# Loads held back until x is turned, and step 0's MLP continued by halves

## The chip, the cores and the metric

The kernel runs on one core of a Trainium2 chip. Its time is the device time of one execution in microseconds (us). Five engines run their own instruction queues in order: PE (matrix products), DVE and ACT (elementwise work), POOL (here small set-up work and the issue of software DMAs) and SP (the issue of hardware DMAs). They meet through semaphores. In the profile, "PEld" is PE's weight load, and "SPq" or "POOLq" is the issuing side of a queue.

## The reference

Windowed attention with sink tokens, and then an MLP with a rational activation, on the joined heads:

```python
batch, n_heads, seq, head_dim = (4, 8, 768, 64);  n_sink, window = (4, 128)
n_tokens, d_model, d_ff = (3072, 512, 2048)

scores = scale * np.matmul(q, k.transpose(0, 1, 3, 2))
keep = is_sink | ((rel >= 0) & (rel < window))     # rel = query position - key position
a = softmax(np.where(keep, scores, -1e9))
x = np.matmul(a, v)                                # as [B * S, H * D]

h = x @ w_in
P = a[0] + a[1] * h + a[2] * h**2 + a[3] * h**3
Q = 1.0 + np.abs(b[0]) * np.abs(h) + np.abs(b[1]) * h**2
out = (P / (Q + 1e-06)) @ w_out                    # float32, [3072, 512]
```

## The kernel before

The 3072 tokens are cut into 12 steps of 256 tokens (`TS`), three steps to a batch. A step s has an attention part and an MLP part, and the attention of later steps runs beside the MLP of earlier ones, about two steps ahead.

**Attention of a step.** POOL issues the loads, cast from float32 to bfloat16 on the way: two of k (`load_k`, L171, 128 KB each), two of q (`load_q`, L155), and eight of v, one a head (`load_v`, L179, 32 KB each). From step 3 on (from the seventh tile on for q) k and q are transposed by DMA, issued from SP: `turn_k_tile` (L335) into `kT_flat`, `turn_q` (L318) into `qT`; in the first steps PE does it. DVE spreads k into a block form (`spread_k`, L364). PE makes the scores of four head pairs (`scores`, L414) and of the sink tokens (`sink_scores`, L381), ACT takes the exponentials (`exps`, L432), DVE masks (`mask`, L439; in the first three steps PE adds the mask), PE multiplies with v in three units (`attend`, L468), and DVE divides (`normalize`, L481) into `x_n`. Then x is transposed into `xblk` in two halves: in steps 0 to 2 by PE (L492) and a copy on ACT (`place_x`, L501), from step 3 on by two DMA transposes from SP (`turn_x_half`, L504). A transposed k buffer has three copies, `v_bd` three, `k_bf` and `xblk` two each, `q_bf` four.

**MLP of a step.** `project_in` (L516) makes h in four quarters of 16 matmuls, copied out by ACT (`copy_in`, L523). Then, on 128 x 4096 elements: absolute values (`magnitude`, L546), squares (`square`, L540 on DVE, L538 on ACT), the denominator (`denominator`, L551), its reciprocal as exp(-ln) on ACT (`log_den`, L577; `recip_den`, L583), and on DVE `even` (L557), `odd` (L562), `odd_h` (L567), `numerator` (L571) and `gate` (L589), whose result g goes into `project_out` (L613): two tiles of tokens, each in two parts of 8 matmuls that need one half of g and one half of `w_out`. ACT copies out (`copy_out`, L618) and SP stores (`store`, L622). The denominator, the logarithm and the exponential go by halves of d_ff in each step; `even` to `gate` go over the whole width, except in the last step, which does them by halves too.

**The order.** The order of every engine's instructions is written by a planner in the kernel. Each operation is a `piece` with an engine, an estimated length, a rank, and a list of pieces that it follows. `run_list` (L900) plays a clock through: an engine that is free takes the able piece of the lowest rank. Where PE has nothing to do in that plan, it adds dummy matmuls (`spin`, L373), which multiply the identity into the bank of the scores. What comes out is a fixed order for each engine; on the chip each queue waits at its head for its own semaphores. The ranks of a step's loads are

```python
        r_ = 4 * s - 20
        ...
            piece(("load_v", s, h), "POOL", 0.62, r_ + 1.0, lambda s=s, h=h: load_v(s, h),
                  [("attend", s - 2, 2)] if s >= 3 else [("ones", s)], kind="sw", load=0.32)
```

and `w_out`'s 16 loads have the ranks -8.0 (the first eight) and -4.5. A load follows only what frees its buffer: k of a step follows the transposes of k two steps before, q those of q two steps before, v the attention two steps before.

Of the kernel before, what the change touches and what calls it, by code (L numbers as in the profile page):

```python
# [10 lines left out]
BF16 = mybir.dt.bfloat16  # L11
# [6 lines left out]
def kernel(  # L18
# [13 lines left out]
    nc = tc.nc  # L32
# [6 lines left out]
    P = 128  # L39
    DM = moe_w_in.shape[0]  # L40
    DF = moe_w_in.shape[1]
    NDMC = DM // P
    NFFC = DF // P
    NPB = H // 2
    TS = 256
    GPB = S // TS
    NSTEP = B * GPB
# [5 lines left out]
    MW = NFFC * TS  # L53
    HW = MW // 2
    NQ_HW = NTS + 1
# [119 lines left out]
    def load_v(s, h):  # L175
        b, g = divmod(s, GPB)
        v_bd[s] = v_fix[s % 3]
        i, e = divmod(h, 2)
        nc.gpsimd.dma_start(  # L179
            out=v_bd[s][e * 64:(e + 1) * 64, i, :, e, 0:D],  # L180
            in_=v[b, h, g * TS:(g + 1) * TS, :].rearrange("(j p) d -> p j d", p=64))
# [321 lines left out]
    def turn_x_half(s, grp):  # L503
        nc.sync.dma_start_transpose(  # L504
            out=x_half(s, grp).rearrange("p (u c) -> p u c", c=P),
            in_=x_n[s][:, 4 * grp * P:4 * (grp + 1) * P])


    hb, sq, den, num, g_of, lnq, ps_h, ps_out, o_t = {}, {}, {}, {}, {}, {}, {}, {}, {}

# [125 lines left out]
    def piece(name, eng, length, rank, run, after=(), takes=None, frees=None, lat=0.0, kind=None,  # L636
              load=0.0):
        w = Piece()
        w.name, w.eng, w.length, w.rank, w.run = name, eng, length, rank, run
        w.after = [a_ for a_ in after if a_ is not None]  # L640
        w.takes, w.frees, w.lat, w.kind, w.load = takes, frees, lat, kind, load
        w.order = len(work)
        assert name not in work
        work[name] = w
# [8 lines left out]
        return name + (s,) if 0 <= s < NSTEP else None  # L653


    piece(("load_k2",), "SP", 0.6, -22, load_k2, kind="hw", load=1.3)
    piece(("load_q3",), "SP", 0.6, -21, load_q3, kind="hw", load=2.8)
    for s in range(NSTEP):
        b, g = divmod(s, GPB)
        r_ = 4 * s - 20  # L660
        if s:
            for t in range(NTS):
                piece(("load_k", s, t), "POOL", 0.9, r_, lambda s=s, t=t: load_k(s, t),
                      [("turned_k", s - 2)] if s > 2 else [], kind="sw", load=0.88)
            for n in range(2 * s + 1, min(2 * s + 3, NQT)):
                piece(("load_q", n), "POOL", 0.9, r_ + 0.5, lambda n=n: load_q(n),
                      [("turn_q", n - 4) if n - 4 >= NQ_HW else None], kind="sw", load=0.88)
        for h in range(H):
            piece(("load_v", s, h), "POOL", 0.62, r_ + 1.0, lambda s=s, h=h: load_v(s, h),
                  [("attend", s - 2, 2)] if s >= 3 else [("ones", s)], kind="sw", load=0.32)  # L670
    for half in range(2):
        for c in range(NDMC):
            piece(("load_w_in", half, c), "POOL", 0.55, -18.9 + half * 3.6,
# [69 lines left out]
    for s in range(NSTEP):  # L743
# [19 lines left out]
        else:  # L763
# [5 lines left out]
        qts = [("place_q3", 1) if n < NQ_HW else ("place_q" if n < NQ_PE else "turn_q", n)  # L769
               for n in range(NTS * s, min(NTS * s + NTS + 1, NQT))]  # L770
        piece(("sink_scores", s), "PE", 0.45, 4 * s + 1 - 8 + 0.35, lambda s=s: sink_scores(s),
              [("spread_k", GPB * b)] + qts, takes="ps_m")
        piece(("sink_exps", s), "ACT", on_act(TS), 4 * s + 1 - 8 + 0.4, lambda s=s: sink_exps(s),
              [("sink_scores", s), ("attend", s - 2, 2) if s >= 2 else None], frees="ps_m")
        if g == 0:
# [44 lines left out]

    SQ_ACT = (4, 7, NSTEP - 1)
    RS = {0: 4.0, 1: 2.0}
    for m in range(NSTEP):
        r_ = 4 * m - RS.get(m, 0)
        old = m - 2
        for j in range(4):
            piece(("gemm1", m, j), "PE", 1.72, r_ + j, lambda m=m, j=j: project_in(m, j),
                  [("turned_x", m)] + [("load_w_in", j // 2, c) for c in range(NDMC)],
                  takes="ps_h")
            piece(("copy_in", m, j), "ACT", on_act(GW), r_ + j + 0.25,  # L830
                  lambda m=m, j=j: copy_in(m, j),
                  [("gemm1", m, j), ("odd_h", old) if old >= 0 and j == 0 else None], frees="ps_h")
        first, second = [("copy_in", m, 0), ("copy_in", m, 1)], [("copy_in", m, 2), ("copy_in", m, 3)]
        piece(("and", m, 0), "DVE", 0.6, r_ + 2.5, lambda m=m: magnitude(m, A_),
              first + ([("gate", old)] if old >= 0 else []))
        eng, how = ("ACT", "act") if m else ("DVE", "dve")
        piece(("sq", m, 0), eng, on_act(HW) if m else on_dve(HW, 2), r_ + 3.9,
              lambda m=m, how=how: square(m, A_, how), first + ([("num", old)] if old >= 0 else [("cast_k2",)]))
        piece(("and", m, 1), "DVE", 0.6, r_ + 4.2, lambda m=m: magnitude(m, B_),
              second + [("and", m, 0)])  # L840
        if m not in SQ_ACT:
            piece(("sq", m, 1), "DVE", on_dve(HW, 2), r_ + 4.25, lambda m=m: square(m, B_, "dve"),
                  second + [("sq", m, 0)])
        else:
            piece(("sq", m, 1), "ACT", on_act(HW), r_ + 4.25, lambda m=m: square(m, B_, "act"),
                  second + [("sq", m, 0)])
        for hf, part in ((0, A_), (1, B_)):
            piece(("den", m, hf), "DVE", on_dve(HW, 2), r_ + 4.35 + hf * 0.85,
                  lambda m=m, part=part: denominator(m, part), [("and", m, hf), ("sq", m, hf)])
            piece(("ln", m, hf), "ACT", on_act(HW, 0.2), r_ + 5.2 + hf,  # L850
                  lambda m=m, part=part: log_den(m, part),
                  [("more_scalars",), ("den", m, hf), ("exp", m - 1, hf) if m else None])
            piece(("exp", m, hf), "ACT", on_act(HW), r_ + 7.2 + hf,
                  lambda m=m, part=part: recip_den(m, part), [("ln", m, hf)])

        last = m == NSTEP - 1
        for hf, part in ((0, A_), (1, B_)) if last else ((None, None),):
            w_ = HW if last else MW
            x_ = 0.0 if hf is None else 1.5 * hf
            halves = (0, 1) if hf is None else (hf,)  # L860
            own = (m,) if hf is None else (m, hf)
            piece(("even",) + own, "DVE", on_dve(w_, 4, 0.12), r_ + 6.2 + x_,
                  lambda m=m, part=part: even(m, part),
                  [("sq", m, h_) for h_ in halves] + [("gate", m - 1) if m else ("cast_q3", 1)])
            piece(("odd",) + own, "DVE", on_dve(w_, 4, 0.12), r_ + 6.9 + x_,
                  lambda m=m, part=part: odd(m, part),
                  [("even",) + own] + [("den", m, h_) for h_ in halves])
            piece(("odd_h",) + own, "DVE", on_dve(w_, 2), r_ + 7.5 + x_,
                  lambda m=m, part=part: odd_h(m, part), [("odd",) + own])
            piece(("num",) + own, "DVE", on_dve(w_, 2), r_ + 7.6 + x_,  # L870
                  lambda m=m, part=part: numerator(m, part), [("odd_h",) + own])
            piece(("gate",) + own, "DVE", on_dve(w_, 2), r_ + 9.3 + x_,
                  lambda m=m, part=part: gate(m, part),
                  [("num",) + own] + [("exp", m, h_) for h_ in halves]
                  + ([("gemm2", m - 2, NTS - 1, 1)] if m >= 2 else
                     [("turned_k", 0), ("turn_q3", 1)]))
        for tt in range(NTS):
            bank = out_bank(m, tt)
            shared = bank == "ps_h"
            for part in range(2):  # L880
                f0, f1 = part * NFFC // 2, (part + 1) * NFFC // 2
                r2 = 0.5 * tt + 1.5 * part if last else 2 * tt + part
                piece(("gemm2", m, tt, part), "PE", 1.73, r_ + 10.6 + r2,
                      lambda m=m, tt=tt, f0=f0, f1=f1: project_out(m, tt, f0, f1),
                      [("gate", m, part) if last else ("gate", m)]
                      + [("load_w_out", c) for c in range(f0, f1)]
                      + ([("gemm2", m, tt, 0)] if part else [])
                      + ([("gemm2", m, 0, 0)] if shared and tt else []),
                      takes=None if part or shared and tt else bank)
            n = NTS * m + tt  # L890
            piece(("copy_out", m, tt), "ACT", on_act(DM), r_ + 12.8 + 2 * tt - 0.2,
                  lambda m=m, tt=tt: copy_out(m, tt),
                  [("gemm2", m, tt, 1), ("copy_out", m, 0) if shared and tt else None, ("store",) + divmod(n - 2, NTS) if n >= 2 else None],
                  frees=None if shared and not tt else bank)
            piece(("store", m, tt), "SP", 0.6, r_ + 12.8 + 2 * tt, lambda m=m, tt=tt: store(m, tt),
                  [("copy_out", m, tt)], kind="hw", load=0.7)
# [125 lines left out]
```

The softmax here doesn't subtract the row's maximum and nothing guards it: scores larger than these inputs give would overflow.

## Time and profile before

| | us |
|---|---|
| median of 5 runs | 272.29 |
| lowest and highest | 269.85, 273.75 |
| the profiled execution | 272.29 |
| its span | 270.6 |
| PE, DVE, ACT, POOL busy | 247.3, 230.4, 224.3, 121.6 |

The profile is of one execution. The span runs from the first to the last instruction; the rest of that execution's time, 1.7 us, lies around it. Busy times are sums over the span. A wait is listed with what ended it; the chain is followed back from the last instruction to what released it, step by step. PE's dummy matmuls count as busy: 395 of them are in the span, 30.1 us by their durations, which overlap.

### The profile page before, as it was taken

The numbers are of one execution on the slowest core, as the hardware profiler recorded it, in microseconds if no ns is written. First come the engines' busy times: TensorE is split into PE (matmuls) and PEld (weight loads), VectorE is DVE, ScalarE is ACT, GpSimd is POOL, SyncE is SP. The second block draws the span as 40 slices with busy tenths as digits, with TensorE's granted clock in tenths as the row PEclk, the third lists the DMA queues.
The fourth block names the chain that finished last, engine by engine and source line by source line (L and its number), as shares of the span: only waits on it lengthen the run. The fifth ranks groups of instructions, "written<-read, shape, count | busy, mean of one in ns | idle before, by whom it ended". The sixth has DMA issues, their size and how long they took to land.

```text
span 270.6 us, 5649 instructions
## 1 busy us (share of the span) xinstructions
PE 247.3 (91%) x2294; PEld 188.8 (70%) x2315; DVE 230.4 (85%) x293; ACT 224.3 (83%) x216; POOL 121.6 (45%) x178
## 2 busy tenths in 40 slices
PE   5899878998989759997989999999999999999994
PEld 5799777885776449877766777867858777675442
DVE  7975189869996298999998999999989999999950
ACT  8643858499979818799999999999999999899831
POOL 8945889799696496493924013290000000000000
PEclk9999999999999979999999999999999999999999
DMA  7999999999999999999995344491030211110222
GB/s 195 99 161 193 64 99 112 168 150 166 135 159 138 125 183 211 138 151 144 157 122 105 37 70 58 31 102 46 19 98 7 73 41 58 39 60 0 81 78 78
DMA packets 109674, 28.07 MB, mean 104 GB/s; under 512 B 101456, under 2 KB 105552, under 8 KB 109648
## 3 DMA queue, kind: packets, MB, share of 16 engines
q0 software_dynamic: 74288, 12.99, 73.7%
q1 hardware_dynamic: 35360, 14.72, 29.5%
q8 instruction: 18, 0.29, 0.5%
q14 instruction: 8, 0.07, 0.1%
HBM read 27.30 MB, written 6.29 MB: 124 GB/s over the span
## 4 chain that ended last, share of the span: by engine, by line
PE 54%; DMA 15%; ACT 9%; POOL 8%; DVE 6%; issue 4%; SPq 3%; ACTq 0%; POOLq 0%
PE ps_out L613 22%; PE ps_h L516 20%; DMA w_in_sb<-in_moe_w_in_dram 6%; PE ps_o L468 5%; DMA q_bf<-in_q_dram 4%; POOL v_bd L179 3%; PE ps_s L373 3%; PE ps_s L414 3%; DMA qT<-q_bf 3%; DMA xblk<-x_n 2%; ACT lnq L577 2%; ACT e L432 2%; SPq L318 2%; POOL w_out_sb L188 1%; ACT sq L538 1%
## 5 line engine op out<-in xcount | busy, mean ns | idle before, releaser
L516 PE MATMUL ps_h<-xblk,w_in_sb 128*128 128x256 bf16 x768 | 91.3, 275 | 4.8 <-DMA xblk<-x_n 4.6
L613 PE MATMUL ps_out<-w_out_sb,g 128*128 128x512 bf16 x363 | 86.8, 379 | 1.8 <-ACT o_t L618 0.6
L516 PEld LDWEIGHTS <-w_in_sb 128*128 128x128 bf16 x768 | 75.0, 99 | 17.8 <-issue 4.8
L179 POOL DMA_DIRECT2D v_bd<-in_v_dram x96 | 63.2, 681 | 45.0 <-PE ps_o L468 30.4
L613 PEld LDWEIGHTS <-g 128*128 128x128 bf16 x384 | 36.6, 98 | 37.0 <-issue 0.9
L523 ACT ACTIVATE hb<-ps_h 128x1024 bf16<-128x1024 f32 x48 | 49.7, 1042 | 12.9 <-PE ps_h L516 12.6
L577 ACT ACTIVATE lnq<-den,one_eps,qsc 128x2048 f32<-128x2048 bf16 x24 | 50.6, 2113 | 1.7 <-DVE den L551 1.6
L583 ACT ACTIVATE den<-lnq 128x2048 bf16<-128x2048 f32 x24 | 46.5, 1939 | 0.0
L432 ACT ACTIVATE e<-ps_s 128x768 bf16<-128x768 f32 x48 | 39.8, 834 | 7.0 <-PE ps_s L420 4.4
L373 PE MATMUL ps_s<-ident 128*128 128x128 bf16 x395 | 30.1, 226 | 6.8 <-ACT e L432 5.4
L551 DVE TENSOR_TENSOR den<-den,sq 128x2048 bf16<-128x2048 bf16 x24 | 29.1, 1220 | 3.1 <-ACT sq L538 2.8
L373 PEld LDWEIGHTS <-ident 128*128 128x128 bf16 x395 | 25.7, 102 | 8.3 <-issue 5.7
L468 PE MATMUL ps_o<-v_bd,e 128*128 128x130 bf16 x352 | 28.5, 219 | 0.1
L589 DVE TENSOR_TENSOR g<-num,den 128x4096 bf16<-128x4096 bf16 (+1 forms) x13 | 27.6, 2121 | 0.6 <-ACT den L583 0.5
L571 DVE TENSOR_TENSOR num<-num,sq 128x4096 bf16<-128x4096 bf16 (+1 forms) x13 | 27.6, 2122 | 0.1
L567 DVE TENSOR_TENSOR sq<-sq,hb 128x4096 bf16<-128x4096 bf16 (+1 forms) x13 | 27.6, 2120 | 0.1
L538 ACT ACTIVATE sq<-hb 128x2048 bf16<-128x2048 bf16 x14 | 27.1, 1938 | 0.1
L468 PEld LDWEIGHTS <-e 128*128 128x128 bf16 x352 | 24.5, 97 | 2.8 <-ACT e L432 0.2
L414 PE MATMUL ps_s<-qT,kT 128*128 128x192 bf16 x192 | 23.8, 246 | 1.8 <-DMA qT<-q_bf 1.2
L618 ACT ACTIVATE o_t<-ps_out 128x512 f32<-128x512 f32 x24 | 14.5, 614 | 12.3 <-PE ps_out L613 8.1
L171 POOL DMA_DIRECT2D k_bf<-in_k_dram x22 | 21.0, 967 | 5.9 <-DMA kT_flat<-k_bf 5.0
L155 POOL DMA_DIRECT2D q_bf<-in_q_dram x21 | 20.7, 996 | 5.1 <-DMA qT<-q_bf 4.6
(84 smaller groups left out, 239.0 us busy)
## 6 DMA issues: line engine op xcount, KB each, us to landing
out_dram<-o_t SPq DMA_DIRECT2D x24, 256.0 KB, 2.6
v_bd<-in_v_dram POOLq DMA_DIRECT2D x96, 32.0 KB, 4.6
k_bf<-in_k_dram POOLq DMA_DIRECT2D x22, 128.0 KB, 6.0
q_bf<-in_q_dram POOLq DMA_DIRECT2D x21, 128.0 KB, 6.3
w_in_sb<-in_moe_w_in_dram POOLq DMA_DIRECT2D x8, 256.0 KB, 8.5
w_out_sb<-in_moe_w_out_dram POOLq DMA_DIRECT2D x16, 128.0 KB, 5.1
stage_q<-in_q_dram SPq DMA_DIRECT2D x1, 768.0 KB, 6.3
stage_kv<-in_k_dram SPq DMA_DIRECT2D x1, 512.0 KB, 4.2
```

The source lines that it names most:

```text
L179: nc.gpsimd.dma_start(out=v_bd[s][e * 64:(e + 1) * 64, i, :, e, 0:D], in_=v[b, h, g * TS:(g + 1) * TS, :].rearrange("(j p) d -> p j d", p=64))
L373: nc.tensor.matmul(ps_scores[:, 0, 384:384 + P], lhsT=ident, rhs=ident, start=True, stop=True)
L414: nc.tensor.matmul(ps[:, n // 2, (n % 2) * 192:(n % 2) * 192 + 192], lhsT=kT_fix[s % 2][:, i * NHF + n, :], rhs=qT_fix[b % 2][:, i, c:c + ...
L432: nc.scalar.activation(out=data.rearrange("p (a n) c -> p a n c", a=2), in_=ps[:, :, 0:384].rearrange("p a (n c) -> p a n c", n=2), func=A ...
L468: nc.tensor.matmul(ps_o[:, u - u0, :], lhsT=l_, rhs=r_.rearrange("p e c -> p (e c)"), start=(m == 0), stop=(m == len(terms) - 1))
L516: nc.tensor.matmul(ps[:, n, :], lhsT=w_in_sb[c][:, fc * P:(fc + 1) * P], rhs=xblk[m][:, c, :], start=(c == 0), stop=(c == NDMC - 1))
L523: nc.scalar.activation(out=hb[m][:, j * GW:(j + 1) * GW], in_=ps_h.pop((m, j)).rearrange("p n c -> p (n c)"), func=AF.Copy)
L538: nc.scalar.activation(out=sq[m][:, c], in_=hb[m][:, c], func=AF.Square)
L551: nc.vector.tensor_tensor(out=den[m][:, c], in0=den[m][:, c], in1=sq[m][:, c], op=ALU.add)
L577: nc.scalar.activation(out=lnq[m, part], in_=den[m][:, c], func=AF.Ln, scale=qsc, bias=one_eps)
L583: nc.scalar.activation(out=den[m][:, c], in_=lnq[m, part], func=AF.Exp, scale=-1.0)
L613: nc.tensor.matmul(ps_out[m, tt], lhsT=g_of[m][:, co:co + P], rhs=w_out_sb[fc], start=(fc == 0), stop=(fc == NFFC - 1))
```

## The change

It has three parts.

1. A new piece, `touch`, for steps 0 to 8: a GpSimd copy of four elements (one partition) of `xblk` of that step into a scratch tile, which follows both transposes of x of that step. From step 4 on, the loads of k and q of step s follow the touch of step s - 4; from step 3 on, the loads of v follow the touch of step s - 3, and their rank is 2.6 higher than it was (`4 * s - 16.4` in place of `4 * s - 19`). POOL's queue is in order, so in the queue these loads stand behind the touch.
2. In step 0, too, `even` to `gate` are done by halves, and each part of the output product follows its half of g.
3. In the plan the sink scores of a step follow the last attention unit two steps before.

```diff
+    scratch = const_pool.tile([P, 4], BF16, name="scratch")
+
+    def touch_x(s):
+
+        nc.gpsimd.tensor_copy(out=scratch[0:1].rearrange("p (a b) -> p a b", a=2),
+                              in_=xblk[s][0:1, 0:NDMC:2, 0:TS:P])
...
+    LEAD = 4
+    for s in range(NSTEP - LEAD + 1):
+        piece(("touch", s), "POOL", 0.15, 4 * s - 9, lambda s=s: touch_x(s), [("turned_x", s)])
...
         r_ = 4 * s - 20
+        rv = r_ + 1.0 if s < LEAD - 1 else 4 * s - 16.4
         if s:
             for t in range(NTS):
                 piece(("load_k", s, t), "POOL", 0.9, r_, lambda s=s, t=t: load_k(s, t),
-                      [("turned_k", s - 2)] if s > 2 else [], kind="sw", load=0.88)
+                      [("turned_k", s - 2) if s > 2 else None,
+                       ("touch", s - LEAD) if s >= LEAD else None], kind="sw", load=0.88)
             for n in range(2 * s + 1, min(2 * s + 3, NQT)):
                 piece(("load_q", n), "POOL", 0.9, r_ + 0.5, lambda n=n: load_q(n),
-                      [("turn_q", n - 4) if n - 4 >= NQ_HW else None], kind="sw", load=0.88)
+                      [("turn_q", n - 4) if n - 4 >= NQ_HW else None,
+                       ("touch", s - LEAD) if s >= LEAD else None], kind="sw", load=0.88)
         for h in range(H):
-            piece(("load_v", s, h), "POOL", 0.62, r_ + 1.0, lambda s=s, h=h: load_v(s, h),
-                  [("attend", s - 2, 2)] if s >= 3 else [("ones", s)], kind="sw", load=0.32)
+            piece(("load_v", s, h), "POOL", 0.62, rv, lambda s=s, h=h: load_v(s, h),
+                  [("attend", s - 2, 2) if s >= 3 else ("ones", s),
+                   ("touch", s - LEAD + 1) if s >= LEAD - 1 else None], kind="sw", load=0.32)
...
         piece(("sink_scores", s), "PE", 0.45, 4 * s + 1 - 8 + 0.35, lambda s=s: sink_scores(s),
-              [("spread_k", GPB * b)] + qts, takes="ps_m")
+              [("spread_k", GPB * b), ("attend", s - 2, 2) if s >= 2 else None] + qts,
+              takes="ps_m")
...
+    BY_HALF = (0, NSTEP - 1)
...
         last = m == NSTEP - 1
-        for hf, part in ((0, A_), (1, B_)) if last else ((None, None),):
-            w_ = HW if last else MW
+        by_half = m in BY_HALF
+        for hf, part in ((0, A_), (1, B_)) if by_half else ((None, None),):
+            w_ = HW if by_half else MW
...
-                      [("gate", m, part) if last else ("gate", m)]
+                      [("gate", m, part) if by_half else ("gate", m)]
```

Since the planner plays its clock with the new pieces, the order changes in many places. On SP, the transposes around step 3's x stood in the order k(5), q(11), q(12), x(3, first half), k(6), q(13), q(14), x(3, second half). They now stand in the order k(5, first tile), x(3, first half), q(11), q(12), k(5, second tile), x(3, second half), q(13), q(14), k(6). On POOL, the last eight loads of `w_out` now stand ahead of the v loads of step 3, and the v loads of step 4 ahead of the k loads of step 5.

More of the change, by code (lines that the diff above doesn't have):

```diff
@@ L876 @@
                      [("turned_k", 0), ("turn_q3", 1)]))
+        if by_half:
+            for name in ("odd_h", "num", "gate"):
+                piece((name, m), "NONE", 0.0, 0, None, [(name, m, h_) for h_ in range(2)])
         for tt in range(NTS):
```

## The prediction

> **What bounds the kernel now.** Names: x(s,g) is the transpose of half g of the attention output of step s (L504), k(s,t) and q(n) are the transposes at L335 and L318, all three from SP. I read first the page's busy rows and slices, then the waits, the chain, the PE timeline at the largest wait, and the table by stage.
>
> ```profile
> span 270.6 us, 5649 instructions
> PE 247.3 (91%) x2294; PEld 188.8 (70%) x2315; DVE 230.4 (85%) x293; ACT 224.3 (83%) x216; POOL 121.6 (45%) x178
> PE   5899878998989759997989999999999999999994
> PEclk9999999999999979999999999999999999999999
> DMA  7999999999999999999995344491030211110222
> ```
>
> PE is the fullest engine. It has two soft places: the start, and slices 13 and 14 (88 to 101 us), where its clock drops too. The DMA engines are full until slice 20 (142 us) and light after.
>
> ```profile
> PE ps_h L516 <- DMA xblk<-x_n: 4.6, 1, 4.6
> DVE kT L364 <- DMA kT_flat<-k_bf: 4.9, 2, 4.7
> ACT o_t L618 <- DMA out_dram<-o_t: 4.2, 1, 4.2
> ```
>
> These waits (total, times, longest) fall together: three engines wait for DMAs at about 90 to 98 us. The chain and the PE timeline say what came last.
>
> ```profile
> 84.28 1.25 SPq L335
> 85.62 1.73 SPq L335
> 87.44 2.86 SPq L318
> 90.39 1.22 SPq L318
> 91.70 6.14 DMA xblk<-x_n
> 97.89 8.22 PE ps_h L516 x62
> ...
> 92.91 0.38 PE L516 MATMUL ps_h<-xblk,w_in_sb 128*128 128x256 bf16 x2
> 97.89 8.22 PE L516 MATMUL ps_h<-xblk,w_in_sb 128*128 128x256 bf16 x62 [4.60 <-DMA xblk<-x_n]
> ```
>
> x(3,1) was issued at 91.70, behind k(6,0), k(6,1), q(13), q(14), and took 6.14 us to land. Step 3's first product then ran 62 matmuls in 8.22 us; elsewhere 32 take 3.49 us on this chain (0.109 each), so 62 should take 6.76. The stall cost 4.60 + 1.46 us.
>
> ```profile
> core 0: us, PE busy (x) PEld busy (x) DVE busy (x) ACT busy (x) POOL busy (x), PEclk, DMA share, GB/s
> 110.00:130.00 20.00, 18.32 (x197) 15.30 (x196) 19.79 (x24) 18.67 (x18) 12.34 (x16) 1.00 1.95 144
> 150.00:170.00 20.00, 19.89 (x171) 15.19 (x171) 19.71 (x22) 19.70 (x19) 3.75 (x6) 1.00 0.35 51
> 210.00:230.00 20.00, 19.89 (x167) 14.50 (x167) 19.33 (x23) 19.98 (x18) 0.00 (x0) 1.00 0.19 55
> ```
>
> From 150 us on PE, DVE and ACT are all 97 to 100% busy. Nothing there can absorb a loss, and what all three gain before then should reach the end.
>
> **What the Trainium skill says.** "DMA: Bandwidth & Descriptors", section "Issuing engines are not separate DMA queues": DMAs from GpSimd and SP run on the same 16 engines and interleave. The trace agrees: transposes of turned x land in 3.4 us at the median, but the four issued between 82 and 99 us took 6.1 to 6.8 where landings are known, with POOL loads beside them. "Perfetto Trace Analysis", section on the HWDGE DMA instruction: the profiled interval of such a DMA ends with its issue, not with its data; 1.22 us of issue against 6.14 to landing above, so I count landings. "TensorE: Matmul & The Clock Gate", Part 1: an idle window of about 3.4 us halves the clock. The trace agrees: 4.60 idle, then the slow 62; waits of 1.4 us (at 36 us) left no such trace.
>
> **The change part by part.**
>
> *Step 0 by halves.* On DVE, five instructions become ten. Halves of the three products take 1217 to 1222 ns against 2284 for a whole (0.15 us more a pair), halves of the two scalings 0.81 against about 1.38 (0.24 more): 3 × 0.15 + 2 × 0.24 = 0.9 us. The first four halves (0.81 + 0.81 + 1.22 + 1.22 = 4.06 us) fit into a 5.48 us hole at 28.3 to 33.8, where DVE waits for step 1's attention, so they are free; were that hole gone they would cost their own 4 us. The second halves: from 41.3, with the two gates and a normalisation between them, g is whole at about 49.4 instead of 53.4. But the first output product of step 0 starts at 58.51 with PE busy before it, so g was not what it waited for. On PE itself, in the new order, the products of step 1 move ahead of one attention unit, and a turn of x moves ahead of ten or so dummy matmuls: I take 0.5 us (0 to 1).
>
> *The weights.* Loads of w_out 8 to 15 move ahead of step 3's eight v loads. Before, the last w_out landed at 64.1 and the second half of that output product began at 63.95; now about 59. The v loads are wanted at about 67 and issued by 60.8. Nothing is lost.
>
> *The touches.* Nine copies of four elements on one partition. No row shows one; nearest are memsets of 128x1 (0.10 us) and an affine select of 128x8 (0.20). I take 0.2 each (0.1 to 0.4), 1.8 us on a POOL that is 45% busy. They hold what stands behind them: k and q loads of step s+4, v loads of step s+3. Touches 0 to 2 find x turned or nearly so (the copy for step 2 ended at 66.96; POOL comes at about 67). Touch 3 waits for x(3,1), and then k(7), q(15), q(16), which POOL issued at 80.1 to 93.4, wait until then. That takes 4 loads of 128 KB out of the crowd around x(3,1), and as many per step later.
>
> *The queues.* POOL: all as before to q(10) (65.2 us); then eight v loads of step 4 stand ahead of k(5): 8 × 0.63 + a touch 0.2 + half of the 2.3 us of waits that they had = 6.3, so k(5) is issued at 71.5 to 73.2 (before: 65.1 to 67.6), q(11), q(12) by 75.0. Such loads landed in 4.2 to 7.2 us in this stretch; I take 5 to 5.5. SP: its new order is k(5,0), x(3,0), q(11), q(12), k(5,1), x(3,1), and only then q(13), q(14), k(6). k(5,0) can go at 76.5, and at 1.25 to 1.3 each x(3,1) is sixth: 76.5 + 5 × 1.25 = 82.8. Its source (third unit of step 3) is written by 82.2 or earlier. Landing 3.4 to 6.8 later; DMA work is still thick, so I take 5.9: 88.7.
>
> *PE there.* In the new order step 3's first product stands ahead of work that before was done by 92.9: two attention units of step 4 (0.85 + 0.57), an output half-tile of step 1 (2 × 1.73), three score products (3 × 0.33) = 5.87. So PE comes at 92.91 - 5.87 = 87.0 or a little less, with some 30 dummy matmuls in front, and waits under 2 us, too little to lose the clock. The sink scores of step 5, just ahead, need q(11) and q(12), which go by 81.5 and land by about 87 as well. To compare: before, with the slow clock added and that work and two early matmuls (0.22) taken out, 97.89 + 1.46 - 5.87 - 0.22 = 93.3; now 88.7. **Gain 4.6 us**; 6 if it lands at 87.3, 2.5 at 90.8. The 0.5 above is within this: the wait swallows it.
>
> *Afterwards.* Before, PE spends 85 dummy matmuls (4.8 us) and some 3 us of idle time between 120 and 147, behind a DVE that is 99% busy (110 to 130). DVE no longer loses 4.7 us to k(6), which now lands at about 93 when DVE comes at about 94. I take 1.2 us of those 7.8 (0 to 3.5). The added order of the sink scores behind an attention is the plan's own and costs nothing while PE has other work.
>
> Sum: 4.6 + 1.2 = 5.8. The profiled execution took 272.29 us, its span 270.6 and 1.7 around it; it is also the median of the five. 272.3 - 5.8 = **266.5 us** (span 264.8).
>
> **Rivals.** (1) *The stall only moves.* Up to q(14) POOL issues the same loads in both kernels, so the engines are as full when x(3,1) goes; if it lands at 93 or later PE waits 6 us again, with the slow clock. For it: share of DMA 2.44 in 76 to 92. Against: four fewer transposes and four fewer loads ahead of it. 93.3 - 93 = 0: 272. (2) *DVE or ACT keeps the time.* Both are full from 150 on; if the new order leaves them only half the gain, 272.3 - 2.9 = 269.4. For it: ACT 99.9% busy in 210 to 230. Against: ACT idles 4.2 + 1.8 us around 94 to 101 for the same cause. (3) *Slower: the loads come too late, in a ring.* Landing of x(s) releases four loads, whose q transposes stand ahead of x(s+1,1) on SP. Ring: touch 0.2 + loads 3.6 + landing 4.3 + two transposes 2.5 + own issue 1.2 + landing 3.4 = 15.2 us, against a step of 17.1 (the chain starts the products of steps 7 and 11 at 167.03 and 235.50). With landings as slow as at 81 us (9.8) and 99 us (6.8) it is 24.1, 7 over. It decides from 17.1 us on; at 18.9, five steps (4 to 8) lose 1.8 each: 272.3 - 5.8 + 9 = 275.5. Against: thinner traffic means landings as at 61 us (4.2).
>
> **How the numbers follow.** Forecast 0.60, (1) 0.12, (2) 0.16, (3) 0.12. The forecast's own range is 263 to 269. About 1% (2.7 us) is what a measurement of this kernel can tell from no change: faster is under 269.6. The forecast and two thirds of (2) are faster (0.70); the rest of (2) and (1) are within (0.17); (3) and an edge of (1) slower (0.13). The range reaches to (1): 263.0 to 272.8.
>
> **What would show it.** Right: x(3,1) issued near 83 and landed by 90; no PE wait over 3 us for turned x and no slow clock after 80; DVE's 4.7 us wait for k(6) gone; POOL idle before each touch from the fourth on. Wrong: waits of PE for turned x or q in steps 4 to 8 (rival 3), a DVE or ACT idle of the old size at another place (1), or a stall that is gone while PE idles more behind them (2).

## The result, and the profile after

The changed kernel takes 273.11 us (median of 43 runs, 269.8 to 276.5); the kernel before 272.14 (80 runs, 269.2 to 276.2). The ratio is 1.0024, 95% interval 1.0005 to 1.0042: no gain, where 266.5 us was forecast. Here and below a median is over all runs, while a ratio and its interval leave out the runs over 1.5% above the kernel's fastest, so the two can differ in the third digit. The profiled execution took 273.09 us, its span 271.4.

The page of the changed kernel:

```profile
span 271.4 us, 5660 instructions
PE 249.9 (92%) x2286; PEld 191.2 (70%) x2306; DVE 233.1 (86%) x298; ACT 224.6 (83%) x216; POOL 128.0 (47%) x187
PE   5999968894999899989998999999999999999994
PEclk9999979999799999999999999999999999999999
DMA  6999899999999999999899997975201211110222
```

The soft place at 88 to 101 us, with its slow clock, is gone. A new one stands in slice 9, counted from 0 (61 to 68 us), where PE is at 4 of 10, with the clock at 7 in the slice behind it. A smaller one, with the clock at 7 too, is in slice 5 (34 to 41 us): PE waits 2.16 us there for k(2). That one belongs to this execution; the kernels below with v first and with `w_out` cut, which are the same up to there, keep their clock. The waits (total, times, longest) name what is behind the one in slice 9:

```profile
PE ps_s L414 <- DMA qT<-q_bf: 3.4, 2, 2.3
DVE kT L364 <- DMA kT_flat<-k_bf: 3.7, 1, 3.7
POOL scratch L512 <- DMA xblk<-x_n: 24.9, 5, 5.7
POOL w_out_sb L188 <- DMA w_out_sb<-in_moe_w_out_dram: 3.7, 4, 1.4
POOL v_bd L179 <- DMA w_out_sb<-in_moe_w_out_dram: 3.1, 2, 1.6
```

PE waits for turned q, not for turned x. POOL, which issues the loads, now waits for `w_out` itself. The chain (start, length, what) and PE's timeline at that place:

```profile
47.48 8.97 DMA q_bf<-in_q_dram
...
56.46 1.19 SPq L318
...
57.74 9.05 DMA qT<-q_bf
...
66.83 0.33 PE ps_s L414 x2
67.15 2.92 PE ps_out L620 x8
```

```profile
65.34 0.34 PE L414 MATMUL ps_s<-qT,kT 128*128 128x192 bf16 x2 [2.25 <-DMA qT<-q_bf]
66.83 0.33 PE L414 MATMUL ps_s<-qT,kT 128*128 128x192 bf16 x2 [1.15 <-DMA qT<-q_bf]
```

The load of q(7) takes 8.97 us, the transpose of q(8) 9.05; the scores of step 3 wait 2.25 + 1.15 us, and the eight matmuls behind them take 2.92 instead of 1.73 (slow clock). That is 4.6 us; the stall that went cost 4.60 + 1.46 = 6.1, counted in the same way. Why q is late shows in the same stretch of POOL's queue, first in the kernel before, then in the changed one:

```profile
49.34 0.55 POOL L188 DMA_DIRECT2D w_out_sb<-in_moe_w_out_dram  x1 [0.33 <-DMA w_out_sb<-in_moe_w_out_dram]
50.48 1.26 POOL L179 DMA_DIRECT2D v_bd<-in_v_dram  x2 [0.59 <-PE ps_o L468]
52.46 3.97 POOL L179 DMA_DIRECT2D v_bd<-in_v_dram  x6 [0.71 <-PE ps_h L516]
56.40 1.12 POOL L188 DMA_DIRECT2D w_out_sb<-in_moe_w_out_dram  x2
57.78 3.04 POOL L188 DMA_DIRECT2D w_out_sb<-in_moe_w_out_dram  x5 [0.26 <-DMA v_bd<-in_v_dram]
60.79 1.80 POOL L171 DMA_DIRECT2D k_bf<-in_k_dram  x2
```

```profile
50.15 0.56 POOL L188 DMA_DIRECT2D w_out_sb<-in_moe_w_out_dram  x1 [0.89 <-DMA w_out_sb<-in_moe_w_out_dram]
51.85 1.07 POOL L188 DMA_DIRECT2D w_out_sb<-in_moe_w_out_dram  x2 [1.15 <-DMA w_out_sb<-in_moe_w_out_dram]
...
55.28 1.14 POOL L188 DMA_DIRECT2D w_out_sb<-in_moe_w_out_dram  x2 [1.40 <-DMA w_out_sb<-in_moe_w_out_dram]
...
58.16 2.47 POOL L179 DMA_DIRECT2D v_bd<-in_v_dram  x4 [0.29 <-PE ps_h L523]
62.13 1.42 POOL L179 DMA_DIRECT2D v_bd<-in_v_dram  x2 [1.50 <-DMA w_out_sb<-in_moe_w_out_dram]
65.15 1.22 POOL L179 DMA_DIRECT2D v_bd<-in_v_dram  x2 [1.60 <-DMA w_out_sb<-in_moe_w_out_dram]
67.30 1.77 POOL L171 DMA_DIRECT2D k_bf<-in_k_dram  x2 [0.94 <-DMA v_bd<-in_v_dram]
69.06 1.77 POOL L155 DMA_DIRECT2D q_bf<-in_q_dram  x2
```

Between the first of these `w_out` loads, which is w_out 8 in both kernels, and k(4) stand the same sixteen loads, and in the changed kernel one touch of 0.18 us. So seven loads of `w_out` moved, 9 to 15. Before, POOL gets through them in 60.79 - 49.34 = 11.45 us; now in 67.30 - 50.15 = 17.15. The loads themselves land later too: w_out 9 to 15 took 3.6 to 4.3 us from issue to landing before and 6.3 to 7.9 now, so that the last of them, issued 3 us earlier, lands at 65.2 instead of 64.1. k(4), q(9) and q(10), next on POOL, are 5.6 to 6.5 us later than before, and SP's queue for step 3 is late with them:

```profile
82.02 1.19 SPq L335 DMA_TRANSPOSE kT_flat<-k_bf  x1
83.39 1.19 SPq L504 DMA_TRANSPOSE xblk<-x_n  x1
84.67 2.62 SPq L318 DMA_TRANSPOSE qT<-q_bf  x2
87.38 1.22 SPq L335 DMA_TRANSPOSE kT_flat<-k_bf  x1
88.69 1.23 SPq L504 DMA_TRANSPOSE xblk<-x_n  x1
```

The order is the forecast one; each entry comes 5.5 to 6 us after its forecast time. PE at step 3's product:

```profile
94.23 1.39 PE L373 MATMUL ps_s<-ident 128*128 128x128 bf16 x22
95.46 1.98 PE L523 MATMUL ps_h<-xblk,w_in_sb 128*128 128x256 bf16 x16
```

x(3,1) took 6.7 us to land, until 95.4. PE comes out of its dummy matmuls at that moment: it doesn't wait because it is as late as x. By stage, first the line of the kernel before for 60 to 75 us, then the changed kernel:

```profile
core 0: us, PE busy (x) PEld busy (x) DVE busy (x) ACT busy (x) POOL busy (x), PEclk, DMA share, GB/s
60.00:75.00 15.00, 13.72 (x130) 10.24 (x131) 14.32 (x17) 14.38 (x15) 12.74 (x17) 1.00 1.84 152
60.00:75.00 15.00, 10.92 (x93) 7.49 (x91) 8.84 (x12) 9.95 (x10) 10.74 (x17) 0.89 1.50 106
150.00:170.00 20.00, 19.90 (x177) 15.26 (x178) 19.74 (x23) 19.38 (x19) 14.70 (x18) 1.00 1.49 121
210.00:230.00 20.00, 19.84 (x174) 14.88 (x176) 18.65 (x21) 19.35 (x19) 0.00 (x0) 1.00 0.18 51
```

From 150 us on it is nearly as full as before (93 to 100%). At 60 to 75 us all three engines lose: DVE is busy for 8.84 us instead of 14.32.

### The profile page after: what moved, and what is told of

Read it like the earlier page. It is cut to its first block, busy times and chain, and to the rows that moved or that the text cites. A ratio compares the mean times of both kernels' runs of the same rounds, so it can differ in the third digit from the quotient of the medians.

```text
span 271.4 us, 5660 instructions
## 1 busy us (share of the span) xinstructions
PE 249.9 (92%) x2286; PEld 191.2 (70%) x2306; DVE 233.1 (86%) x298; ACT 224.6 (83%) x216; POOL 128.0 (47%) x187
## 4 chain that ended last, share of the span: by engine, by line
PE 31%; DVE 19%; ACT 18%; DMA 17%; issue 7%; POOL 5%; another core or an unknown queue 1%; SPq 0%; ACTq 0%; POOLq 0%
PE ps_out L620 12%; PE ps_h L523 12%; DMA w_in_sb<-in_moe_w_in_dram 7%; ACT den L590 5%; ACT hb L530 4%; DMA qT<-q_bf 3%; DMA q_bf<-in_q_dram 3%; PE ps_o L468 3%; ACT lnq L584 3%; POOL v_bd L179 3%; DVE sq L574 3%; ACT e L432 2%; DMA k_bf<-in_k_dram 2%; DVE x_n L481 2%; ACT sq L545 2%
## 5 line engine op out<-in xcount | busy, mean ns | idle before, releaser
L620 PE MATMUL ps_out<-w_out_sb,g 128*128 128x512 bf16 x364 | 87.8, 383 | 1.6 <-ACT o_t L625 0.6
L432 ACT ACTIVATE e<-ps_s 128x768 bf16<-128x768 f32 x48 | 39.1, 819 | 10.1 <-PE ps_s L414 4.9
L373 PE MATMUL ps_s<-ident 128*128 128x128 bf16 x386 | 30.7, 233 | 6.6 <-ACT e L432 4.8
L373 PEld LDWEIGHTS <-ident 128*128 128x128 bf16 x386 | 26.9, 107 | 7.3 <-issue 4.5
L171 POOL DMA_DIRECT2D k_bf<-in_k_dram x22 | 21.6, 991 | 1.9 <-DMA v_bd<-in_v_dram 0.9
L414 PEld LDWEIGHTS <-kT 128*128 128x128 bf16 x192 | 16.9, 99 | 7.4 <-DMA qT<-q_bf 2.4
L481 DVE SCALAR_TENSOR_TENSOR x_n<-ps_o,csc,rec 128x384 bf16<-128x384 f32 (+1 forms) x36 | 20.6, 573 | 1.3
```

Of the source, the lines that this page charges most:

```text
L373: nc.tensor.matmul(ps_scores[:, 0, 384:384 + P], lhsT=ident, rhs=ident, start=True, stop=True)
L414: nc.tensor.matmul(ps[:, n // 2, (n % 2) * 192:(n % 2) * 192 + 192], lhsT=kT_fix[s % 2][:, i * NHF + n, :], rhs=qT_fix[b % 2][:, i, c:c + ...
L432: nc.scalar.activation(out=data.rearrange("p (a n) c -> p a n c", a=2), in_=ps[:, :, 0:384].rearrange("p a (n c) -> p a n c", n=2), func=A ...
L620: nc.tensor.matmul(ps_out[m, tt], lhsT=g_of[m][:, co:co + P], rhs=w_out_sb[fc], start=(fc == 0), stop=(fc == NFFC - 1))
```

## Experiments

Theory: the changed load order (`w_out` 9 to 15 ahead of step 3's v) makes q(7), q(8) and POOL's queue late, and this takes the gain. Rivals: DVE and ACT keep the time whatever PE does ("bound"); the halves or the touches cost it; the early waits do. The third part of the change, the sink scores behind an attention unit, stays in every kernel made from the changed one and isn't priced by itself. "Exchange" below means this edit, which leaves every engine's order as planned and swaps places on POOL alone (here v first; the other way round in the second kernel):

```diff
+    order = run_list()
+    moved = [("load_v", 3, h) for h in range(H)] + [("load_w_out", c) for c in range(9, NFFC)]
+    slots = [i_ for i_, w in enumerate(order) if w.name in moved]
+    for i_, name in zip(slots, moved):
+        order[i_] = work[name]
-    for w in run_list():
+    for w in order:
```

| kernel | median us | ratio to before | 95% interval |
|---|---|---|---|
| changed | 273.11 | 1.0024 | 1.0005, 1.0042 |
| changed, v first | 271.22 | 0.9964 | 0.9932, 0.9995 |
| before, w_out first | 274.55 | 1.0109 | 1.0049, 1.0169 |
| changed, q first | 275.25 | 1.0136 | 1.0063, 1.0208 |
| changed, no halves | 273.35 | 1.0031 | 0.9996, 1.0065 |
| changed, w_out cut | 269.46 | 0.9890 | 0.9860, 0.9919 |
| before, w_out cut | 271.28 | 1.0009 | 0.9983, 1.0035 |
| touches and halves | 269.53 | 0.9908 | 0.9879, 0.9937 |
| touch-only | 267.03 | 0.9824 | 0.9774, 0.9875 |
| touch-only, second set | 266.94 | 0.9814 | 0.9753, 0.9875 |
| touch-only, w_out first | 268.99 | 0.9927 | 0.9900, 0.9954 |
| before and halves | 270.06 | 0.9938 | 0.9909, 0.9967 |
| no halves, v first | 270.24 | 0.9950 | 0.9924, 0.9976 |

**The exchange in both kernels.**

> The changed kernel, every engine's order kept, but on POOL the eight v loads of step 3 exchange places with the loads of w_out 9 to 15, so that they stand ahead again as in the kernel before. Crowding (my theory: the weights beside them make q(7) and q(8) late): latencies of q(7), q(8) loads fall from 8.7-9.0 to 6.5-7.1 us and of their transposes from 8.8-9.1 to 5-6; PE's 3.4 us wait for q goes, with the slow clock after it; 267.5 to 269.5 us. Bound (rival: DVE and ACT keep the time whatever PE does): the wait goes and the time stays at 272 to 274. Early loss (rival: the 2.2 us wait for k(2) and the touch ahead of the last w_in load made PE late already): q no longer late but the time falls by no more than 1 us.

> The kernel before, every engine's order kept, but w_out 9 to 15 exchange places with the v loads of step 3 and stand ahead, as in the changed kernel. Crowding: q(7), q(8) loads and transposes take 8 to 9 us each instead of 5 to 7, PE waits 2 to 4 us for q at about 65 us, and the stall of step 3's product shrinks by what PE comes later, so the time grows by 0 to 4 us (272 to 276). If the weights don't crowd q: no wait for q over 1 us, latencies as before, 271.5 to 272.8 us.

With `w_out` first, the kernel before gets the changed kernel's stall at the changed kernel's place, and 1.1% (3.0 us):

```profile
64.06 0.34 PE L414 MATMUL ps_s<-qT,kT 128*128 128x192 bf16 x2 [2.68 <-DMA qT<-q_bf]
65.49 0.48 PE L414 MATMUL ps_s<-qT,kT 128*128 128x192 bf16 x2 [1.09 <-DMA qT<-q_bf]
```

The transpose of q(7) took 8.6 us there; in the kernel before 5.1, in the changed one 8.8. The stall at step 3's product stays beside it, smaller (2.69 us, at 101.34). With v first the changed kernel has q in time (5.0 us) and gains 0.6%, less than I expected, because PE's planned order now uses `w_out` 9 to 15 before they land:

```profile
63.10 0.38 PE L620 MATMUL ps_out<-w_out_sb,g 128*128 128x512 bf16 x1 [0.48 <-DMA w_out_sb<-in_moe_w_out_dram]
63.81 0.38 PE L620 MATMUL ps_out<-w_out_sb,g 128*128 128x512 bf16 x1 [0.34 <-DMA w_out_sb<-in_moe_w_out_dram]
64.53 0.38 PE L620 MATMUL ps_out<-w_out_sb,g 128*128 128x512 bf16 x1 [0.34 <-DMA w_out_sb<-in_moe_w_out_dram]
65.28 0.38 PE L620 MATMUL ps_out<-w_out_sb,g 128*128 128x512 bf16 x1 [0.38 <-DMA w_out_sb<-in_moe_w_out_dram]
66.07 0.58 PE L620 MATMUL ps_out<-w_out_sb,g 128*128 128x512 bf16 x1 [0.41 <-DMA w_out_sb<-in_moe_w_out_dram]
...
66.88 0.84 PE L414 MATMUL ps_s<-qT,kT 128*128 128x192 bf16 x4
```

Five matmuls wait for one load each, and the slow clock follows (four score matmuls in 0.84 us; 0.49 at full clock). In the changed plan PE comes to the second half of step 0's output product at 61.5 us, soon after the first; in the plan before it came at 63.95, and `w_out` at 64.1. So the change asked the DMA engines for q and for `w_out` at about 62 us; either order makes one of them late.

**q first.**

```diff
+    moved = [("load_q", 7), ("load_q", 8)] + [("load_w_out", c) for c in range(8)]
```

> The changed kernel, every engine's order kept, but on POOL the loads of q(7) and q(8) exchange places with w_out 0 to 7 and stand ahead of them, 4 to 5 us earlier. Crowding: the transposes of q(7), q(8) are issued about 4 us earlier, q is there when PE comes, the wait of 3.4 us goes; w_out 0 to 7 come 1.5 us later, still before 58 us; 267.5 to 270 us. Bound: 272 to 274 with the wait gone. Early loss: less than 1 us faster.

Slower still, 275.25 us: a miss. q is there, and from 60 to 75 us PE, DVE and ACT are busy again (13.7, 13.3 and 14.5 of 15). The loss comes behind: at 78.83 the scores of step 4 wait 1.97 us for DVE's spread of k, and at 95.59 step 3's product 2.10 us for x, with a slow clock in between. POOL came to k(4) at 64.37, after 60.79 in the kernel before, but ahead of the changed kernel's 67.30. Why this ends slower than the changed kernel stays open; that q in time isn't enough, it shows.

**Fewer bytes in the same places.**

```diff
-        nc.gpsimd.dma_start(out=w_out_sb[c], in_=moe_w_out[c * P:(c + 1) * P, :])
+        rows = P if c < 8 else 8
+        nc.gpsimd.dma_start(out=w_out_sb[c][0:rows], in_=moe_w_out[c * P:c * P + rows, :])
...
-rhs=w_out_sb[fc],
+rhs=w_out_sb[fc % 8],
```

> The changed kernel, every order kept; the loads of w_out 8 to 15 fetch 8 of their 128 rows, and the output products read w_out 0 to 7 in their place. This takes 8 loads of 128 KB out of the DMA engines at 50 to 60 us and leaves the order and the number of issues alone. Supply: q(7), q(8) loads land in 6.5 to 7.5 us, their transposes in 5 to 6, PE's wait of 3.4 us and the slow clock behind it go, and no other wait replaces them: 266 to 268.5 us, the time that I had forecast. Bound: 271 to 273 with the waits gone.

> The same cut of w_out 8 to 15 in the kernel before. Supply: nothing waits for these loads there, and the stall at 98 us comes from SP's queue and from loads issued after 70 us, so it stays at 3 to 5 us: 270.5 to 272.5 us, so that the changed kernel with the same cut is 3 to 5 us faster than this one. If loads issued at 50 to 60 us push everything later, so that the whole queue comes forward: 268 to 270 and the stall is smaller.

This kernel leaves out 120 of 128 rows of these loads and multiplies with other rows in their place. The changed kernel gains 1.3 points of ratio and has no wait for q left, and POOL comes to k(4) at 61.55 instead of 67.30; the kernel before gains nothing and keeps its stall (3.34 us at 97.69). With this cut, the change is worth (1.0009 - 0.9890) × 272 = 3.2 us. That speaks against "bound": a supply cut of loads at 50 to 60 us reaches the end. It is a little short of the 266 to 268.5 expected; PE still waits 1.92 us for x at 91.48.

**The halves.**

```diff
-    BY_HALF = (0, NSTEP - 1)
+    BY_HALF = (NSTEP - 1,)
```

> The changed kernel without step 0 by halves (the planner orders the rest anew, touches and places of v as changed). My prediction priced the halves at a gain of 0.5 us (0 to 1), so 273 to 274 here. If the halves are what costs (ten DVE instructions for five, attention units shifted on PE): 270 to 271. If the crowding is all, w_out still stands ahead and the wait for q stays at 2 to 4 us.

No difference from the changed kernel (1.0031 to 1.0024). The halves are not what took the gain. But PE's wait for q is only 1.64 us here, less than expected and with the clock full, and the kernel is no faster for it. Nor is the wait always 3.4 us with the halves: two runs below that leave out touches and keep this load order show 1.82 and 1.97 us. So the 4.6 us above are one execution's, and the late q isn't the whole loss.

**Step 3's loads at their old rank, planned anew.**

```diff
-        rv = r_ + 1.0 if s < LEAD - 1 else 4 * s - 16.4
+        rv = r_ + 1.0 if s < LEAD else 4 * s - 16.4
...
-                   ("touch", s - LEAD + 1) if s >= LEAD - 1 else None], kind="sw", load=0.32)
+                   ("touch", s - LEAD + 1) if s >= LEAD else None], kind="sw", load=0.32)
```

> The changed kernel with step 3's v loads at their old rank and without their touch (the other touches, the halves and the sink scores stay), and the planner orders all anew: the v loads stand ahead of w_out 9 to 15, and on PE the second half of step 0's output product comes later again, behind three score products, an attention unit and two pieces of step 2's product. Unlike the run with the places exchanged on POOL alone, PE then meets neither a late q nor a late w_out. Supply (my theory now: at 45 to 70 us the DMA engines cannot deliver both q(7), q(8) and w_out 8 to 15 by the time at which the changed order uses them): no DMA wait of PE over 1.2 us between 55 and 80 us, clock full there, 267 to 269 us. Bound (rival: DVE and ACT keep the time): 271 to 273 with PE's waits gone.

> As the run before it, and without step 0 by halves: what is left of the change is the touches from step 4's k and q loads and step 4's v loads on. PE's order to 90 us is then that of the kernel before. Supply: the stall of 4.6 us and its slow clock at 98 us shrinks to under 2 us and nothing is lost ahead of it: 267 to 269 us. Halves count: if the halves are worth what I predicted (0.5 us), 0 to 1 us slower than the run before it. Bound: 271 to 273.

> Once more the kernel with the touches and the halves and step 3's v loads at their old place, whose six runs lay between 264.8 and 273.6 us, beside kernels of the same set. If the halves cost nothing: 266 to 268, as without them. If they cost what the medians so far say: 269 to 271.

The first of the three was too scattered to read: 264.8 to 273.6 in six runs, median 270.1, and a ratio of 0.9798 (0.9708 to 0.9889) that rests on two of them. Its repetition gives 269.5, slower than the 267 to 269 expected. Without the halves ("touch-only") it is 267.0 us, 1.8% faster than before and the best version found. (It also keeps the later rank of v from step 4 on and the order of the sink scores.) It differs from the kernel without halves (273.35 us) in these two lines alone: (1.0031 - 0.9824) × 272 = 5.6 us. Its step 3:

```profile
90.66 1.22 SPq L504 DMA_TRANSPOSE xblk<-x_n  x1
...
92.67 5.27 SPq L504 DMA_TRANSPOSE xblk<-x_n  x2
```

```profile
93.80 0.38 PE L523 MATMUL ps_h<-xblk,w_in_sb 128*128 128x256 bf16 x2
94.76 6.93 PE L523 MATMUL ps_h<-xblk,w_in_sb 128*128 128x256 bf16 x62 [0.58 <-DMA xblk<-x_n]
```

The 62 matmuls end at 101.69; before, they ended at 106.11, on the same PE order. x(3,1) is issued only a microsecond earlier than before (90.66; it was 91.70) and still behind k(6), q(13), q(14), but lands by 94.76, in 4.1 us instead of 6.14. Two things differ beside it: the transposes of k(7), which stood right behind it, now come behind x(4), and the loads of k(7), q(15), q(16) and, through the touch, of the next v come later. Without the touches, in the same order, x(3,1) takes 6.5 us (90.19 to 96.69), with v loads beside it; so in these traces the order alone doesn't make it land faster.

**The price of the exchange there, and of the plan.**

> The 267.0 us kernel (touches without the halves, step 3's v loads at their old place), every order kept, but w_out 9 to 15 exchange places with step 3's v loads on POOL, as in the changed kernel. This prices the load order alone in a kernel that has no other loss there. Supply: q(7), q(8) late, PE waits 1.5 to 4 us at 62 to 66, and with the slow clock the time grows by 2.5 to 5 us, 269.5 to 272. Planner (rival: the order that the planner makes after 80 us from the moved ranks costs the rest of the 6 us between this kernel and the one with the moved v loads): only 0 to 2 us slower.

> The changed kernel without the halves (273.4 us), every order kept, but step 3's v loads exchange places with w_out 9 to 15 on POOL and stand ahead. It differs from the 267.0 us kernel only in the order that the planner made of the moved ranks on the other engines (70 lines of PE's order differ). Loads alone: if the exchange is worth what it was in the other pairs (2.8 us) and the plan costs the rest: 270 to 271. Tied together (PE's order assumes the early w_out, so that PE then waits for w_out 9 to 15 instead, as in the same exchange in the changed kernel): 271.5 to 273. If the plan costs nothing: 267 to 268.

With `w_out` first, the touch-only kernel loses 1.0% (2.8 us) by waits of 1.45 and 1.56 us for q at 62.75 and 64.65. With v first, the kernel without halves gains 0.8% (2.2 us). That is the 270 to 271 of "loads alone". Between the latter and touch-only, which have these loads in the same order, 1.3% (3.4 us) remain, and the orders of the other engines are what differs. Which part of these orders costs it isn't shown. One part is seen: PE meets the late `w_out` again (five waits, 1.6 us, and the slow clock after).

**The halves alone.**

```diff
+    BY_HALF = (0, NSTEP - 1)
```

> The kernel before with step 0's products by halves and nothing else of the change. My prediction: a gain of 0.5 us (0 to 1), 271.5 to 272.3 us here. If the order that the planner makes of it costs time (second attention unit of step 1 and the dummy matmuls moved, x turned later): 273 to 276.

A gain of 1.7 us, more than forecast: in that plan PE has attention and output work left in front of step 3's product, which starts at 97.89 without a wait, x(3,1) having landed at 97.5. A smaller stall stays ahead of it (2.71 us at 90.68, for DVE's normalisation, with the slow clock behind it). Halves and touches work on the same stall, and their gains don't add: with the halves, by the repetition above, the touch-only kernel is 0.8 to 0.9% slower (by its ratio, the scattered first set shows no difference). PE there waits 2.14 us at 108.78 for x of step 4.

**The touches themselves.**

```diff
-        if w.run:
+        if w.run and w.name[0] != "touch":
```

> The changed kernel, every order kept, the nine touches left out. If their waits hold back loads that PE then lacks (my rival of the ring, or a cost of the touches themselves): 1 us or more faster, 271 to 272. If their waits protect the transposes of x: 1 to 3 us slower, 274 to 276. If only the order counts: 272.5 to 273.7.

> The same 267.0 us kernel, every order kept, but the nine touches are not issued, so that POOL goes on to the loads behind them as soon as their buffers are free. If it is the order of the queues that brings the gain (x(3,1) ahead of q(13), q(14) and k(6) on SP) and not the waits of the touches: 266 to 268 us, x(3,1) still issued by 84 us. If the waits bring it (loads of step 7 and later held back from the transposes): x lands 2 us or more later in steps 4 to 8 and the time is 269 to 272.

> The touch-only kernel, every order kept, the touches left out, once more, beside the kernel with them on the same chip. Order alone: within 0.7 us of it. Waits count: 1 to 2.5 us slower than it.

> The touch-only kernel again, as the base of this set: 266.5 to 268 us, ratio to the kernel before 0.979 to 0.986.

> The changed kernel, every order kept, without touches 0 and 1. If the cost lies with these two, among the weights' loads: 270 to 271 us, as without all nine. If it lies with the later ones: 272.5 to 273.7. If both early cost and late gain count: under 270.

> The touch-only kernel, every order kept, without touches 0 and 1. The late touches bring the gain: 265.5 to 267.2 us, no slower than with all nine. The early ones do: 268 to 269, as without all.

Touch-only without its touches takes 267.78 us (0.9894) and 268.59 us (0.9893, beside 266.94 with them): some 1.1% comes from the order alone. Another 0.7% may come from the waits, but the intervals overlap. x(3,1) isn't issued by 84 us, as the second text expected, but at 90.19, behind q(13), q(14) and k(6). Without touches 0 and 1 it is 267.84 (0.9837, 0.9803 to 0.9871), between the two forecasts: which touches help isn't told apart. In the changed kernel the sign turns: without any touch 270.44 us (0.9948, 0.9920 to 0.9976), 2 us faster; without the first two 272.78 (1.0062, 1.0020 to 1.0104), no faster. So touches 2 to 8 cost about 2 us there. Through which wait isn't settled: the profiles with and without them differ in several small places. In both of these runs PE comes earlier to step 3's product and waits for x, 1.87 and 1.80 us at 93.8 and 94.0, with the clock full.

## Why the prediction was wrong, step by step

- *The stall at step 3's product*: right in the mechanism, in part by luck in the trace. There is no wait for x, no slow clock after 80 us, and DVE's wait for k(6) is gone. But x(3,1) landed at 95.4, not 88.7, and PE happened to be as late. Where PE is in time, it waits 1.8 to 1.9 us (`w_out` cut, touches left out), within the "under 2 us" forecast. The 3.7 us that DVE still waits are for k(3), until 55.4 us; it waits as long with v first (3.76) and with `w_out` cut (4.33), so that isn't the load order's. That the stall is worth 4 to 5 us the touch-only kernel shows (4.4 at the end of that product, 4.8 to 5.1 in the time).
- *"The weights ... Nothing is lost"*: the step that failed. I asked only whether `w_out` and v come by when they are used, and took it that loads issued earlier land earlier: the last `w_out` at about 59 (it was 65.2, after 64.1 before), v issued by 60.8 (it was 66.4). Seven loads moved, not eight; w_out 8 stood ahead of v already. I didn't ask what runs beside these loads (the transpose of q(7): 5.1 us became 8.8) nor what stands behind them on POOL. Measured: 1.6 to 3.0 us by the exchange in four pairs, and 5.6 with the plan that follows from the moved rank, against nothing in my sum.
- *"POOL: all as before to q(10) (65.2 us)"*: failed by the same cause. The issue of q(10) ended at 70.83. From there the walk carried the error on: k(5) issued at 76.6 to 78.4 (forecast 71.5 to 73.2), x(3,1) at 88.69 (82.8), the product at 95.46 (88.7). The walk's order and spacing held; the landing of x(3,1) took 6.7 us where I took 5.9.
- *The touches*: 0.18 to 0.19 us on POOL for the first three, as taken, but 0.25 to 2.23 for the six behind them, 7.2 us in all by the profile (whose lengths on POOL are rough) where I took 1.8. Their waits aren't free in the changed kernel (2 us); that is the direction of rival 3, without the waits of PE by which I would have known it.
- *The halves*: forecast 0.5 us; 1.7 alone, nothing in the changed kernel. I treated as independent what works on the same stall.
- *Rivals*: "the stall only moves" has the right time and the wrong place: I let it move at x(3,1) only. Rival 2 falls: touch-only has PE, DVE and ACT 99 to 100% busy from 120 to 200 us, and ends 5 us earlier. My own sign for the first rival, "a DVE or ACT idle of the old size at another place", is what the profile shows from 60 to 75 us: DVE is idle 5.5 us more than before and ACT 4.4.
- That 267.0 us of the touch-only kernel is near my 266.5 doesn't confirm the walk: there x(3,1) isn't sixth in SP's queue, it merely lands faster. What I took for afterwards (1.2 us) isn't tested by itself.

## What to carry to other kernels

When loads change places, look at what is on the DMA engines beside them and at what waits behind them on the issuing queue, not only at when they are used; price both even where the load itself has slack. In a kernel with a planner, a moved rank also moves when the consumer comes, so a stall can be fixed in one place and bought back at another; exchanging two groups of loads with every other order kept tells the two apart. Gains that work on the same stall don't add.

## What the runs showed of the hardware

The same sixteen loads took POOL 11.45 us with the v loads between (11.74 in touch-only), and 17.15 with w_out 8 to 15 in a row (15.46 in touch-only with the exchange). In the second case POOL waited for landings of earlier loads, up to 1.60 us at a time. A row of eight loads of 128 KB isn't enough for that: w_out 0 to 7, in the same queue of the changed kernel, went out in 5.04 us without a wait, while the eight behind them and behind q(7), q(8) waited. Loads issued earlier can land later: the last of `w_out`, issued 3 us sooner, landed 1.1 us later (65.2, after 64.1).

The clock also fell without one long wait: after 2.25 + 1.15 us, and after five waits of 0.34 to 0.48 us within some 3.5 us. Single waits of 2.26 us (touch-only, at 77.54) and even 3.34 us (the kernel before with `w_out` cut, at 97.69) left it full: 62 matmuls took 6.93 us behind the 3.34, and 8.22 behind the 4.60 in the kernel before. So the length of the longest wait doesn't decide it. The Trainium skill ("TensorE: Matmul & The Clock Gate", Part 1) speaks of a window of about 3.4 us that runs freely. That would fit these figures, if it is the idle share of such a stretch that counts, and where the stretch falls; no run here shows the window itself.
